# Signs that come in through a rectifier's slope, four early units as 64-token visits, and a new order of work, in a retention and feed-forward kernel

## The chip, the cores and the metric

The kernel runs on one core of a Trainium2 chip. The metric is the device time of one execution in microseconds (us), as the median of several runs. The engines are TensorE (PE, with its weight loads shown apart as PEld), VectorE (DVE), ScalarE (ACT), GpSimd (POOL) and SyncE (SP), which here only issues DMAs.

## The reference

A linear attention with decay (retention) over 8 batches, 8 heads, 576 tokens and a head width of 64 is followed by a feed-forward block with a rational activation.

```python
scores = (1 / sqrt(64)) * q @ k.T                      # per batch and head
ret    = scores * where(i >= j, gamma[h] ** (i - j), 0)
x      = (ret @ v) -> [4608 tokens, 512]
h      = x @ w_in                                      # [4608, 2048]
P      = a0 + a1*h + a2*h**2 + a3*h**3
Q      = 1 + |b0|*|h| + |b1|*h**2
out    = (P / (Q + 1e-6)) @ w_out                      # [4608, 512]
```

Attention's inputs are float32. The weights w_in and w_out come as float64 (512 KB a tile); the host only views them as 64-bit integers, and the chip turns each into float32.

## The kernel before, in words

**Tiles.** The 4608 tokens are 36 units of 128 tokens; four units make a block of 512 columns, of which there are 9. The hidden width 2048 is 16 tiles (`f`). One *step* is one pair (block b, tile f), 144 in all, in the order: block 0 with f = 0 to 7, block 1 with f = 0 to 15, block 0 with f = 8 to 15, then blocks 2 to 8. A step's first product (`gemm1`, `h<-xhi,w` and `h<-xlo,w` in the trace, 12 matmuls of 512 columns) makes h; some fifteen elementwise instructions on ACT, DVE and POOL make g = P/Q from it; the second product (`gemm2`, `acc<-w,g`, 12 matmuls) adds g times w_out to an accumulator. Numbers are split in a high and a low part (`xhi`, `xlo`; `w`; `g`), and three of the four partial products are taken.

**Weights.** There are 32 weight tiles (16 of w_in, 16 of w_out, 512 KB each as loaded). `weight()` (lines 262 to 311) converts one: `begin` (ACT) takes the upper word's magnitude scaled as a float32, `digit` (ACT) takes some bits of the lower word, `join` (DVE) shifts and ors them, `sign` (DVE) ors the sign bit in, `high_part` (ACT or DVE) and `low_part` (POOL or DVE) make the two parts. The tiles w_in 0 to 7 and w_out 0 to 7 are needed by steps 0 to 7, the others from step 16 on.

**Attention.** Units 0 to 7 (`EARLY`) are done by `attention()` (lines 398 to 507): 16 score matmuls of 128 columns (`ps<-qk`), a mask over 1024 columns on DVE (`s<-ps,mask_sb`), outputs (`ps<-s,kv`), the state's update (`ps<-kv`) and the old state's share (`ps<-qk,S_sb`). ACT and DVE then keep the result as `xhi` and `xlo`, DVE adds to the state (`S_sb`) and POOL fades it. From unit 8 on a unit is done by `late_visit()` (lines 631 to 709) in two pieces of 64 tokens: the *visit* after unit n computes unit n's outputs and, interleaved with them on the four quarters of the array, unit n+1's scores and state update.

**Order.** Nothing is emitted in the order of the source. Every piece is a `Task` with a due time, an engine (some have a choice of two, with a `HOLD` penalty), a cost and the buffers it takes. `Plan.run()` (lines 121 to 190) repeatedly picks, by a model of the engines' clocks, the task that can begin first, within a `SLACK` the one that is due first, and emits it. The tables of numbers at the top (`LOADS`, `DUE`, `HOLD`, `SLACK`, `FIRST`, `UNITS`, `LATE`) thus set each engine's queue; `LOADS` sets the order of the first DMAs on SP. Each engine runs its queue in order. `WARM` matmuls on zeros (`unread`) run before the first scores. In the first 24 steps (`IN_BANK`) v's line is kept in the PSUM bank of h; `V_POOL` lists the steps whose `v_mul` goes to POOL.

All instructions show line 71 in the trace (the wrapper that emits them), so they are told apart by their tiles.

Of the kernel before, what the change touches and what calls it, by code (L numbers as in the profile page):

```python
# [22 lines left out]
P = 128  # L23
# [23 lines left out]
LOADS = 'w0 0 gq mask 1 w1 gv 2 w2 3 w4 w5 w3 5 4 ab w7 6 w9 w6 w10 w8 7 w11'.split()
# [8 lines left out]
DUE = {'p_begin': 0.5, 'size': 0.727, 'p_mul': 0.7, 'p_mul2': 0.93, 'v_line': 0.797, 'v_mul': 0.806, 'log': 1.578, 'exp': 1.838, 'quot': 1.6, 'check': 1.65, 'better': 0.79, 'g_hi': 1.888, 'g_lo': 2.167, 'gemm2': 3.44, 'begin': -0.243, 'digit': 0.045, 'join': 0.128, 'sign': -0.303, 'high_part': 1.252, 'low_part': 0.8, 'scale_q': -0.354, 'scale_v': -0.5, 'scores': 0.178, 'decay': 0.311, 'outputs': 1.268, 'cross': 0.51, 'keep_hi': 1.415, 'keep_lo': 0.942, 'grow': 0.669, 'fade': 0.87}  # L56
HOLD = {('POOL', 'scale_v'): 3.0, ('DVE', 'p_begin'): 0.616, ('DVE', 'high_part'): 0.5, ('DVE', 'g_hi'): 1.221, ('DVE', 'keep_hi'): 1.153, ('DVE', 'g_lo'): 99.0, ('DVE', 'low_part'): 1.002, ('POOL', 'v_mul'): 0.229}
SLACK = {'PE': 0.19, 'ACT': 0.283, 'DVE': 0.2, 'POOL': 0.006, 'SP': 0.301}

ADJ = {}  # L60

# [39 lines left out]
class Plan:  # L101
# [19 lines left out]
    def run(self):  # L121
# [14 lines left out]
        dma, left, now, reach = 0.0, len(self.tasks), -2.0, REACH  # L136
        while left:
            best = None
            for e, queue in wait.items():
                found = []  # L140
                for t in queue:
# [8 lines left out]
                    s = max(s, clock[e])  # L150
# [43 lines left out]
def retention_ffn(ctx: ExitStack, tc: tile.TileContext, qkv, w_in, w_out, ab, masks, masks2, gq, gv, out):  # L194
# [8 lines left out]
    cnt = ctx.enter_context(tc.tile_pool(name="cnt", bufs=CNT))  # L203
# [13 lines left out]
        "qk": 2, "kv": 2, "xp": 2, "cnv": CNV, "t": CNT, "v": 2, "u": 2, "p": 3, "g": 3, "o0": 1, "o1": 1,  # L217
# [12 lines left out]
    qc = const.tile([P, 1], F32, name="qc")  # L230
# [27 lines left out]
    bits, parts, joins = {}, {}, []  # L258
# [3 lines left out]
    def weight(order, s, w, f, loaded):  # L262
# [7 lines left out]
        def begin():  # L270
            c_[0] = cnv.tile([P, DM], I32, tag="c", name=f"c{nm}")
            act.activation(c_[0].bitcast(F32), words()[1].bitcast(F32), AF.Abs, scale=math.ldexp(1.0, -112))

        def digit():
            c_[1] = cnt.tile([P, DM], I32, tag="t", name=f"t{nm}")
            act.activation(c_[1], words()[2], AF.Copy, scale=15 * 2.0**-17)

        def join():
            dve.scalar_tensor_tensor(c_[0], c_[0], 3, c_[1], ALU.logical_shift_left, ALU.bitwise_or)

        def sign():
            dve.scalar_tensor_tensor(c_[0], words()[1], -0x80000000, c_[0], ALU.bitwise_and, ALU.bitwise_or)
# [16 lines left out]
        def low_part_v():  # L299
# [3 lines left out]
        t = add("ACT", d + DUE["begin"], 0.55, begin, [loaded], [("cnv", k)])  # L303
        t = add("ACT", d + DUE["digit"], 0.55, digit, [t], [("t", k)])
        t = add("DVE", d + DUE["join"], 0.61, join, [t], [], [("t", k)], True)
        joins.append(t)
        t = add("DVE", d + DUE["sign"], 0.61, sign, [t], shared=True)
        hi = add("ACT", d + DUE["high_part"], 0.53, high_part, [t], other=[("DVE", 0.5, high_part_v, True)])
        w_ready[k] = hi, add(
            "POOL", d + DUE["low_part"], 1.21, low_part, [hi], [], [("cnv", k)], True, [("DVE", 0.61, low_part_v, True)]  # L310
# [20 lines left out]
    def load_unit(n, due, after=()):  # L331
# [4 lines left out]
        def of(w, nm):  # L336
# [12 lines left out]
            add("SP", due + 0.01 * w, 524 / 390.0, of(w, nm), after, [] if late else [(nm, n)])  # L349
# [9 lines left out]
    def scale(n, at_, got, consts):  # L359
# [16 lines left out]

    def attention(n, d, gap, got, consts, prev):
# [121 lines left out]
        th = add("ACT", at_(DUE["keep_hi"]), 0.5, keep_hi, done, [("xp", b)] if n % 4 == 0 else [], gives,  # L499
# [518 lines left out]
```

## Time and profile before

| | |
|---|---|
| median of 3 runs | 900.45 us (900.18 to 901.44) |
| span of the profiled execution | 898.8 us (its own time beside the span is not given; the median is 1.65 us longer than the span) |
| PE busy | 882.9 us, 98% |
| DVE / ACT / POOL busy | 788.7 / 652.5 / 163.3 us |
| DMA rate, first three slices of 22.5 us | 343, 406, 407 GB/s; 82 in the fourth |
| granted TensorE clock | 0.999 on the mean |

Busy time is the time in which an engine has an instruction under way. The time lines have a start and a length in us, then engine, operation, written and read tiles, and a count. In square brackets stands the idle time of the engine just ahead and what ended it. A float32 matmul appears as two instructions, so counts are twice those of the source for some shapes.

### The profile page before, as it was taken

Reading aid. Unit: us, or ns where it says so; the run is one execution under the profiler, and the core shown is the slowest. Engines: PE = TensorE matmul, PEld = TensorE weight load, DVE = VectorE, ACT = ScalarE, POOL = GpSimd, SP = SyncE. Lnnn points to the kernel's source line nnn. Section 1 sums busy time; section 2 is a strip of 40 time slices with the busy share of each in tenths; the row PEclk is TensorE's granted clock in tenths of the full one; section 3 lists DMA queues with packets and bytes.
Section 4 is the critical chain, followed back from the end, with each engine's and each line's share of the span. In section 5 each row is a group of like instructions: output and inputs, shape, how many; then the busy total and the mean of one; then the engine's idle time right before and its main releaser. Section 6 shows DMA issues by size and latency. Waiting matters only on the chain.

```text
span 898.8 us, 17725 instructions
## 1 busy us (share of the span) xinstructions
PE 882.9 (98%) x7344; PEld 730.4 (81%) x7344; DVE 788.7 (88%) x1215; ACT 652.5 (73%) x1019; POOL 163.3 (18%) x141
## 2 busy tenths in 40 slices
PE   6999999999999999999999999999999999999998
PEld 5777888888888888888888888888888888888886
DVE  4899999989989998988988888988888888987976
ACT  3589999975667768666766676767676786767765
POOL 2565664522210110011111010001100000000000
PEclk9999999999999999999999999999999999999999
DMA  9992000034311112111211131112211121001001
GB/s 343 406 407 82 1 1 1 1 107 131 105 49 60 53 34 76 41 47 60 95 48 48 59 107 48 48 47 73 81 48 42 27 80 44 1 1 47 1 1 47
DMA packets 22641, 67.41 MB, mean 75 GB/s; under 512 B 2592, under 2 KB 4512, under 8 KB 22560
## 3 DMA queue, kind: packets, MB, share of 16 engines
q1 hardware_dynamic: 22560, 66.28, 20.8%
q8 instruction: 57, 0.93, 0.4%
q14 instruction: 24, 0.20, 0.1%
HBM read 56.83 MB, written 9.44 MB: 74 GB/s over the span
## 4 chain that ended last, share of the span: by engine, by line
PE 94%; DMA 3%; DVE 2%; issue 0%; SPq 0%; ACT 0%; ACTq 0%; DVEq 0%
PE acc L71 44%; PE h L71 43%; PE ps L71 7%; DMA qk<-in_qkv 1%; DMA bits<-in_w_in 1%; DMA gq_sb<-in_gq 1%; DVE p L71 0%; DVE c L71 0%; DVE s L71 0%; DVE xlo L71 0%; DVE w L71 0%; DVE h L71 0%; DVE kv L71 0%; SPq L71 0%; DVE S_sb L71 0%
## 5 line engine op out<-in xcount | busy, mean ns | idle before, releaser
L71 PE MATMUL acc<-w,g 128*128 128x512 f32 x1632 | 394.1, 390 | 0.0
L71 PEld LDWEIGHTS acc<-w,g 128*128 128x128 f32 x1632 | 305.5, 188 | 64.2 <-POOL w L71 0.4
L71 PE MATMUL h<-xhi,w 128*128 128x512 f32 x1152 | 310.5, 392 | 0.3 <-DVE p L71 0.2
L71 PEld LDWEIGHTS h<-xhi,w 128*128 128x128 f32 x1152 | 213.9, 188 | 46.7 <-DVE p L71 1.3
L71 ACT ACTIVATE p<-h,ab_sb 128x512 f32<-128x512 f32 x143 | 110.7, 774 | 86.3 <-PE h L71 84.5
L71 PE MATMUL h<-xlo,w 128*128 128x512 f32 x576 | 154.2, 389 | 0.0
L71 DVE TENSOR_TENSOR p<-p,h 128x512 f32<-128x512 f32 x144 | 98.4, 683 | 55.7 <-ACT u L71 52.7
L71 DVE SCALAR_TENSOR_TENSOR p<-p,ab_sb,h 128x512 f32<-128x512 f32 x168 | 124.6, 744 | 10.6 <-ACT u L71 8.0
L71 PEld LDWEIGHTS h<-xlo,w 128*128 128x128 f32 x576 | 108.1, 188 | 23.0
L71 ACT ACTIVATE g<-p 128x512 fp32r<-128x512 f32 x136 | 85.6, 630 | 50.8 <-DVE p L71 48.3
L71 ACT ACTIVATE u<-v,qc 128x512 f32<-128x512 f32 x120 | 86.7, 723 | 44.7 <-DVE v L71 44.7
L71 ACT ACTIVATE v<-u,absb 128x512 f32<-128x512 f32 x124 | 101.1, 815 | 3.6
L71 DVE SCALAR_TENSOR_TENSOR p<-p,ab_sb,u 128x512 f32<-128x512 f32 x120 | 93.8, 782 | 4.3 <-ACT u L71 4.3
L71 ACT ACTIVATE u<-h 128x512 f32<-128x512 f32 x144 | 84.8, 589 | 11.1 <-DVE v L71 5.3
L71 DVE SCALAR_TENSOR_TENSOR p<-v,p 128x512 f32<-128x512 f32 x120 | 84.4, 703 | 3.8
L71 DVE SCALAR_TENSOR_TENSOR v<-v,u 128x512 f32<-128x512 f32 x120 | 87.1, 726 | 0.0
L71 DVE TENSOR_TENSOR v<-v,u 128x512 f32<-128x512 f32 x120 | 82.8, 690 | 4.3 <-ACT v L71 3.2
L71 DVE TENSOR_TENSOR g<-p,g 128x512 fp32r<-128x512 f32 x112 | 77.5, 692 | 3.8 <-ACT g L71 2.9
L71 ACT ACTIVATE u<-u 128x512 f32<-128x512 f32 x120 | 75.0, 625 | 2.1
L71 POOL TENSOR_TENSOR qk<-qk,gq_sb 128x512 f32<-128x512 f32 x36 | 49.6, 1379 | 92.5 <-DMA qk<-in_qkv 83.9
L71 PEld LDWEIGHTS ps<-qk 64*64 64x64 f32 (+1 forms) x1024 | 38.1, 145 | 19.8 <-issue 10.8
L71 PE MATMUL ps<-qk 64*64 64x64 f32 (+1 forms) x1024 | 43.6, 234 | 8.1 <-POOL qk L71 6.0
(58 smaller groups left out, 738.4 us busy)
## 6 DMA issues: line engine op xcount, KB each, us to landing
qk<-in_qkv SPq DMA_DIRECT2D x36, 512.0 KB, 4.2
kv<-in_qkv SPq DMA_DIRECT2D x36, 512.0 KB, 5.6
bits<-in_w_in SPq DMA_DIRECT2D x16, 512.0 KB, 10.0
bits<-in_w_out SPq DMA_DIRECT2D x16, 512.0 KB, 10.2
out<-o SPq DMA_DIRECT2D x14, 512.0 KB, 3.3
out<-o SPq DMA_DIRECT2D x8, 256.0 KB, 2.2
x<-in_qkv SPq DMA_DIRECT2D x7, 256.0 KB, 5.3
gq_sb<-in_gq SPq DMA_DIRECT2D x1, 256.0 KB, 6.7
```

What stands on the lines that cost most here:

```text
L71: return lambda *a, **k: self.tc.keep_in_program_order(method(*a, **k))
```

## The change

1. **Weights** (`weight`). `begin` becomes a parametric rectifier in place on the upper words: positive words are scaled by 2^-112 as before, negative ones by a further slope of -2^32, which sets a bit that the later shift by 3 moves to the sign's place. `digit` writes in place over the lower words. `join` reads both from `bits`, writes the new tile `c`, and `sign` is gone: one DVE integer instruction a tile where there were two. The buffer `t` of `digit` is gone.
2. **Units 4 to 7** are no longer done by `attention()` but by `late_visit()`, with the accumulators' PSUM banks (`psa`, `psb`) as their room. Only units 0 to 3 (`DENSE`) stay as they were. Between visits to units 3 and 7 the state passes as in the later visits. Unit 7's visit computes outputs only, unit 8's first visit scores only, as before.
3. **Fewer pointers.** `log` takes its bias as a number and not from the tile `qc`; in the first 24 steps `p_begin` and the line of v lose their bias pointer, and a DVE instruction that follows adds the term instead.
4. **Order.** All tables are new; q/k and k/v of an early unit are placed apart in the order of loads; the planner's model of DMA is changed. `WARM` is 18 instead of 8, `V_POOL` has 9 steps instead of 4.

```diff
-V_POOL = range(4)
+DENSE = 4
+VISITS = (-77.42, -41.32, -7.31, -33.57, -0.9)
+V_POOL = (0, 1, 2, 3, 10, 11, 12, 14, 17)
-WARM = 8
+WARM = 18
-LOADS = 'w0 0 gq mask 1 w1 gv 2 w2 3 w4 w5 w3 5 4 ab w7 6 w9 w6 w10 w8 7 w11'.split()
+LOADS = '1 0 mask gq gv 0v 2 1v w1 w0 3 mask2 w2 2v w5 3v 5v w4 4 ab 4v w3 w8 5 6 w11 6v w7 w10 w6 w9 7v 7'.split()
...
         def begin():
+            x = words()[1].bitcast(F32)
+            act.activation(x, x, AF.Prelu, scale=math.ldexp(1.0, -112), alpha=-math.ldexp(1.0, 32))
+
+        def digit():
+            act.activation(words()[0], words()[2], AF.Copy, scale=15 * 2.0**-17)
+
+        def join():
             c_[0] = cnv.tile([P, DM], I32, tag="c", name=f"c{nm}")
-            act.activation(c_[0].bitcast(F32), words()[1].bitcast(F32), AF.Abs, scale=math.ldexp(1.0, -112))
-
-        def digit():
-            c_[1] = cnt.tile([P, DM], I32, tag="t", name=f"t{nm}")
-            act.activation(c_[1], words()[2], AF.Copy, scale=15 * 2.0**-17)
-
-        def join():
-            dve.scalar_tensor_tensor(c_[0], c_[0], 3, c_[1], ALU.logical_shift_left, ALU.bitwise_or)
-
-        def sign():
-            dve.scalar_tensor_tensor(c_[0], words()[1], -0x80000000, c_[0], ALU.bitwise_and, ALU.bitwise_or)
+            dve.scalar_tensor_tensor(c_[0], words()[1], 3, words()[0], ALU.logical_shift_left, ALU.bitwise_or)
...
-    def visit(n):
+    def visit(n, old, new):
         m, heads = n + 1, [(j, g) for j in range(2) for g in range(NPAIR)]
-        if "ps" not in late_s:
+        if m <= EARLY and not (new and m == EARLY):
+            if "early" not in late_s:
+                late_s["early"] = [ps_acc.tile([P, 2, 512], F32, tag="acc", name=f"ps{x}") for x in "ab"]
+                bank["o"], bank["ds"] = late_s["early"][0][:, 0], late_s["early"][0][:, 1]
+            if new:
+                bank["s"] = late_s["early"][1][:, m % 2]
+        elif "ps" not in late_s:
...
-            act.activation(e["p"], hs[key], AF.Identity, bias=a2, scale=a3)
+            if early:
+                act.activation(e["p"], hs[key], AF.Copy, scale=a3)
+            else:
+                act.activation(e["p"], hs[key], AF.Identity, bias=a2, scale=a3)
...
-            dve.tensor_tensor(p, p, hs[key], ALU.mult)
+            if early:
+                dve.scalar_tensor_tensor(p, p, a2, hs[key], ALU.add, ALU.mult)
+            else:
+                dve.tensor_tensor(p, p, hs[key], ALU.mult)
...
-            act.activation(e["r"], e["v"], AF.Ln, bias=qc)
+            act.activation(e["r"], e["v"], AF.Ln, bias=QC)
...
-    for n in range(EARLY):
-        attention(n, FIRST[n], 2, got[n], consts, prev)
+    for n in range(DENSE):
+        masked.append(attention(n, FIRST[n], 2, got[n], consts, prev))
+    late_s["S0"] = S_sb
+    consts["mask2"] = load(begin_of("mask2"), 32, mask2_sb, masks2)
+    prev = {"fade": prev["fade"]}
+    for n in range(DENSE - 1, EARLY):
+        late_visit(n, VISITS[n + 1 - DENSE], got.get(n + 1), consts, prev, masked[-1:] if n < DENSE else [],
+                   n >= DENSE, n + 1 < EARLY)
```

Three places in the engines' queues follow. In the names the figure behind the letters is the unit (`qk5`), block and tile (`h0_1` is block 0, f = 1; `w0_1` is w_in, f = 1, `c1_0` is w_out, f = 0).

PE where the first step begins, before:

```order
L71 MATMUL ps3_309<-qk3_143,S_sb_105 64x128 x8
L71 MATMUL ps5_404<-qk5_157 128x128 x8
L71 MATMUL h0_0_414<-xhi0_251,w0_0_152 128x512 x4
L71 MATMUL h0_0_414<-xlo0_252,w0_0_152 128x512 x4
L71 MATMUL ps4_432<-qk4_161 128x128 x8
L71 MATMUL ps5_404<-s5_424,kv5_159 64x128 x8
L71 MATMUL ps5_404<-kv5_159 64x64 x8
L71 MATMUL h0_0_414<-xhi0_251,w0_0_152 128x512 x4
L71 MATMUL ps4_432<-s4_461,kv4_173 64x128 x8
```

PE at the same place now:

```order
L73 MATMUL ps3_262<-qk3_142,S_sb_104 64x128 x8
L73 MATMUL h0_0_370<-xhi0_216,w0_0_309 128x512 x4
L73 MATMUL h0_0_370<-xlo0_217,w0_0_309 128x512 x4
L73 MATMUL psb_390<-qk4_237 64x64 x16
L73 MATMUL psa_389<-kv4_256 64x64 x8
L73 MATMUL h0_0_370<-xhi0_216,w0_0_309 128x512 x4
L73 MATMUL h0_1_428<-xhi0_216,w0_1_239 128x512 x4
L73 MATMUL h0_1_428<-xlo0_217,w0_1_239 128x512 x4
L73 MATMUL psb_390<-qk5_298 64x64
```

The first step's product now follows unit 3 at once, and units 4 to 7 come as visits of 64-column matmuls between the first products of steps 0 to 5.

DVE from the masks of units 2 and 3 to the low part of unit 3's result, before:

```order
L71 TENSOR_TENSOR s2_304<-ps2_282,mask_sb_98 128x1024
L71 TENSOR_TENSOR s3_339<-ps3_309,mask_sb_98 128x1024
L71 TENSOR_TENSOR kv3_145<-kv3_145,gv_sb_100 128x512
L71 SCALAR_TENSOR_TENSOR c0_2_266<-c0_2_266,t0_2_297 128x512
L71 TENSOR_TENSOR S_sb_105<-S_sb_105,ps2_282 128x256
L71 TENSOR_TENSOR xlo0_252<-ps2_282,xhi0_251 128x4x128
L71 SCALAR_TENSOR_TENSOR c0_2_266<-bits0_2_140,c0_2_266 128x512
L71 SCALAR_TENSOR_TENSOR c1_0_341<-c1_0_341,t1_0_377 128x512
L71 TENSOR_TENSOR S_sb_105<-S_sb_105,ps3_309 128x256
L71 TENSOR_TENSOR xlo0_252<-ps3_309,xhi0_251 128x4x128
```

The same stretch of DVE's queue now:

```order
L73 TENSOR_TENSOR s3_274<-ps3_262,mask_sb_98 128x1024
L73 SCALAR_TENSOR_TENSOR c0_0_296<-bits0_0_140 128x512
L73 TENSOR_TENSOR kv3_193<-kv3_193,gv_sb_100 128x512
L73 SCALAR_TENSOR_TENSOR c0_2_311<-bits0_2_146 128x512
L73 TENSOR_TENSOR S_sb_104<-S_sb_104,ps2_241 128x256
L73 TENSOR_TENSOR xlo0_217<-ps2_241,xhi0_216 128x4x128
L73 TENSOR_TENSOR kv5_197<-kv5_197,gv_sb_100 128x512
L73 SCALAR_TENSOR_TENSOR c1_0_354<-bits1_0_222 128x512
L73 SCALAR_TENSOR_TENSOR c0_4_358<-bits0_4_170 128x512
L73 TENSOR_TENSOR S_sb_104<-S_sb_104,ps3_262 128x256
L73 TENSOR_TENSOR xlo0_217<-ps3_262,xhi0_216 128x4x128
```

Each weight tile has one instruction here where it had two, but four tiles are joined in this stretch instead of parts of two, and unit 5's v is scaled ahead of unit 3's result.

ACT's first instructions, before:

```order
L71 ACTIVATE c0_0_132<-bits0_0_117 128x512
L71 ACTIVATE t0_0_136<-bits0_0_117 128x512
L71 ACTIVATE w0_0_152<-c0_0_132 128x512
L71 ACTIVATE c0_1_198<-bits0_1_129 128x512
L71 ACTIVATE t0_1_205<-bits0_1_129 128x512
L71 ACTIVATE xhi0_251<-ps0_164 128x4x128
```

ACT's first instructions now:

```order
L73 ACTIVATE bits0_1_138<-bits0_1_138 128x512
L73 ACTIVATE xhi0_216<-ps0_149 128x4x128
L73 ACTIVATE bits0_1_138<-bits0_1_138 128x512
L73 ACTIVATE bits0_0_140<-bits0_0_140 128x512 x2
L73 ACTIVATE w0_1_239<-c0_1_225 128x512
L73 ACTIVATE xhi0_216<-ps1_161 128x4x128
```

The first weight is no longer converted ahead of the attention; unit 0's and unit 1's results stand behind weight instructions.

## Rows read from the trace of the kernel before

**Rows 1.** The page, busy time of each engine, and the DMA rate by slice

```profile
PE 882.9 (98%) x7344; PEld 730.4 (81%) x7344; DVE 788.7 (88%) x1215; ACT 652.5 (73%) x1019; POOL 163.3 (18%) x141
...
GB/s 343 406 407 82 1 1 1 1 107 131 105 49 60 53 34 76 41 47 60 95 48 48 59 107 48 48 47 73 81 48 42 27 80 44 1 1 47 1 1 47
```

**Rows 2.** Busy time by stretch: length, PE, PEld, DVE, ACT, POOL, clock, DMA share, GB/s

```profile
100.00:165.00 65.00, 65.00 (x289) 53.83 (x288) 63.60 (x98) 64.09 (x110) 37.95 (x28) 1.00 0.00 1
165.00:285.00 120.00, 119.40 (x1318) 98.59 (x1319) 109.50 (x172) 84.07 (x137) 26.34 (x23) 1.00 0.22 74
```

**Rows 3.** The chain of waits in order of time: start, length, what

```profile
85.81 2.72 PE h L71 x12
```

**Rows 4.** Time line from the start to the first step's product

```profile
1.06 3.79 PE L71 MATMUL unread<-S_sb 128*128 128x128 f32 x16 [1.06 <-DVE qc L71]
...
4.25 0.66 ACT L71 ACTIVATE c<-bits 128x512 f32<-128x512 f32 x1 [2.22 <-DMA bits<-in_w_in]
...
8.93 1.26 POOL L71 TENSOR_TENSOR qk<-qk,gq_sb 128x512 f32<-128x512 f32 x1 [8.47 <-DMA gq_sb<-in_gq]
...
10.24 4.24 PE L71 MATMUL ps<-qk 64*128 64x128 f32 x32 [5.39 <-POOL qk L71]
...
12.37 1.23 DVE L71 TENSOR_TENSOR s<-ps,mask_sb 128x1024 f32<-128x1024 f32 x1 [4.01 <-PE ps L71]
...
31.00 0.68 DVE L71 TENSOR_TENSOR xlo<-ps,xhi 128x512 fp32r<-128x512 f32 x1
...
31.35 1.20 PE L71 MATMUL h<-xhi,w 128*128 128x512 f32 x4
```

**Rows 5.** Time line of PE: one early unit, and where step 8 begins

```profile
46.96 1.09 PE L71 MATMUL ps<-s,kv 128*64 128x128 f32 x16
47.88 0.64 PE L71 MATMUL ps<-kv 128*64 128x64 f32 x16
48.45 1.16 PE L71 MATMUL ps<-qk 64*128 64x128 f32 x16
49.54 1.09 PE L71 MATMUL ps<-qk,S_sb 64*64 64x128 f32 x16
50.56 1.20 PE L71 MATMUL h<-xhi,w 128*128 128x512 f32 x4
...
79.05 1.98 PE L71 MATMUL h<-xhi,w 128*128 128x512 f32 x8
```

**Rows 6.** Time line of PE: first and second late visit

```profile
183.66 1.15 PE L71 MATMUL ps<-qk 64*64 64x64 f32 x32
...
185.21 2.11 PE L71 MATMUL acc<-w,g 128*128 128x512 f32 x8
187.25 0.27 PE L71 MATMUL ps<-qk 64*64 64x64 f32 x1
...
189.28 1.19 PE L71 MATMUL acc<-w,g 128*128 128x512 f32 x4
```

**Rows 7.** DVE by operation: tiles, shape, count, busy us, mean ns, idle before

```profile
L71 DVE TENSOR_TENSOR xlo<-ps,xhi 128x512 fp32r<-128x512 f32 x36 | 24.6, 683 | 1.6 <-ACT xhi L71 1.5
L71 DVE SCALAR_TENSOR_TENSOR c<-bits,c 128x512 int32<-128x512 int32 x32 | 22.9, 717 | 0.2
L71 DVE TENSOR_TENSOR kv<-kv,gv_sb 128x512 f32<-128x512 f32 x32 | 22.7, 711 | 1.3 <-DMA kv<-in_qkv 0.9 <-DMA gv_sb<-in_gv 0.2
...
L71 DVE TENSOR_TENSOR s<-ps,mask_sb 128x1024 f32<-128x1024 f32 x7 | 8.5, 1218 | 4.3 <-PE ps L71 4.3
...
L71 DVE TENSOR_TENSOR S_sb<-S_sb,ps 128x256 f32<-128x256 f32 x6 | 2.5, 415 | 2.7 <-ACT xhi L71 1.4 <-PE ps L71 1.3
```

**Rows 8.** ACT by operation, as in rows 7

```profile
L71 ACT ACTIVATE u<-v,qc 128x512 f32<-128x512 f32 x120 | 86.7, 723 | 44.7 <-DVE v L71 44.7
...
L71 ACT ACTIVATE u<-u 128x512 f32<-128x512 f32 x120 | 75.0, 625 | 2.1
...
L71 ACT ACTIVATE c<-bits 128x512 f32<-128x512 f32 x32 | 21.3, 667 | 11.5 <-DMA bits<-in_w_in 8.2 <-DVE w L71 2.1 <-POOL w L71 1.1
```

More of the change, by code (lines that the diff above doesn't have):

```diff
@@ L135, in run @@
         port = {"DVE": 0.0, "POOL": 0.0}
[L136 removed]
+        dma, landed, left, now, reach = 0.0, [0.75] * OUTSTANDING, len(self.tasks), -2.0, REACH
         while left:
@@ L254, in retention_ffn @@
     first = half + NF
-    bits, parts, joins = {}, {}, []
+    bits, parts = {}, {}
     need = sorted(((at[1, f] if f >= half else f) + 3 * w, w, f) for w in range(2) for f in range(NF))
@@ L302, in weight @@
         d = min(s - LEAD, AHEAD + order)
[L303 to L308, printed above, removed]
+        t = add("ACT", d + DUE["begin"], 0.56, begin, [loaded])
+        t = add("ACT", d + DUE["digit"], 0.56, digit, [t])
+        t = add("DVE", d + DUE["join"], 0.6, join, [t], [("cnv", k)], shared=True)
+        hi = add("ACT", d + DUE["high_part"], 0.52, high_part, [t], other=[("DVE", 0.5, high_part_v, True)])
         w_ready[k] = hi, add(
-            "POOL", d + DUE["low_part"], 1.21, low_part, [hi], [], [("cnv", k)], True, [("DVE", 0.61, low_part_v, True)]
+            "POOL", d + DUE["low_part"], 1.25, low_part, [hi], [], [("cnv", k)], True, [("DVE", 0.6, low_part_v, True)]
         )
@@ L498, in attention @@
         gives = [("acc", key)]
-        th = add("ACT", at_(DUE["keep_hi"]), 0.5, keep_hi, done, [("xp", b)] if n % 4 == 0 else [], gives,
+        th = add("ACT", at_(DUE["keep_hi"]), 0.495, keep_hi, done, [("xp", b)] if n % 4 == 0 else [], gives,
                  other=[("DVE", 0.6, keep_hi_v, False)])
@@ L622, in named, with late_visit @@
         return emit
-    def late_visit(n, d, got, consts, prev, hold):
-        old, m = n >= EARLY, n + 1
-        new, u = m < NU, (n + 1) % 9
+    def late_visit(n, d, got, consts, prev, hold, old=True, new=True):
+        m, u = n + 1, (n + 1) % 9
+        early = m <= EARLY and not (new and m == EARLY)
         tq = tv = None
@@ L646, in late_visit @@
         if m in sooner:
-            tm = add("DVE", d - 1.5, 0.42, named(middle, m), [prev["visit"], prev.get("fade")])
+            tm = add("DVE", d - 1.5, 0.33, named(middle, m), [prev["visit"], prev.get("fade")])
         if n + 2 in sooner:
@@ L662, in late_visit @@
         ts = add(
-            "PE", d, (1.7 if m in sooner and n % 9 != 8 else 2.2) if old and new else 1.2, named(visit, n),
+            "PE", d, (1.7 if m in sooner and n % 9 != 8 else 2.2) if old and new else 1.2, named(visit, n, old, new),
             [tq, tv, tm, te, *hold, *(prev.get(x) for x in ("decay", "middle", "grow", "lo", "before"))],
-            [("h", key)] if new else [],
+            [("acc", "va"), ("acc", "vb")] if early and not old else [("h", key)] if new and not early else [],
         )
```

138 lines of the change are left out of this document (72 added, 66 removed).

## The prediction

> **What bounds the kernel now.** I read the busy times first. PE has work under way for 882.9 of 898.8 us [rows 1], and from step 8 on the chain of waits lists little but PE pieces like the one in [rows 3]: 12 products of 512 columns in 2.72 us, one after the other. So time can be won only by giving PE less to do, or where PE is not full. The table by stretch says where that is not: from 100 to 165 us PE is busy for 65.00 of 65.00, and from 165 to 285 us for 119.40 of 120.00 [rows 2]. In the first of these ACT (64.09) and DVE (63.60) are full as well, so anyone who makes PE arrive earlier must ask whether they can follow. What is left is the start, and there I read the time line. PE's first scores start at 10.24, behind POOL's scaling of q at 8.93, which waited for the DMA of gq; the first step's product starts only at 31.35, behind unit 3's result (its low part is made by DVE at 31.00) [rows 4]. Step 8 starts at 79.05 + 4 x 2.72/12 = 79.96, since the eight products of that row are four of step 7 and four of step 8 [rows 5].
>
> Between 31.35 and 79.96 lie 48.6 us. The work in them: 8 first products and 4 second ones, 12 x 2.72 = 32.6, and units 4 to 7. A unit's pieces start at 46.96, 47.88, 48.45, 49.54 and the next at 50.56 [rows 5]: outputs 0.92, state 0.57, scores 1.09, old state 1.02, in all 3.6. Four make 14.4; unit 4 has its old state on half its columns (0.5 less) and one set of scores (1.1) was done ahead of 31.35, so 12.8. Work 45.4, gaps 3.2.
>
> **Part 1, the head (to the first step's product).** The DMAs run at about 0.28 MB/us from 4.25 us, when the first 0.52 MB are there, to 8.93, when gq closes 1.84 MB (three loads of 512 KB and its own 256), and at the page's 406 GB/s later [rows 1, 4]. With the new loads gq closes 1.48 MB (two of 512 KB, the mask's 160, its own): 4.25 + 0.95/0.28 = 7.7, so 1.2 us sooner, and the first scores start near 9.0.
> The 18 warming products cost nothing or little: 8 of them take 3.79 us [rows 4], 18 at that pace 8.5, to 9.6 us, 0.55 later than 9.0; the pace may rise on the way. I take nothing, since DVE's queue, below, ends later.
> Of the clock: the granted clock of these rows is full, yet the 32 scores from 10.24 took 4.24 us [rows 4], where 16 later take 1.16 [rows 5]. [...]
> DVE's queue from the first mask (12.37) to the end of unit 3's low part (31.68) is 19.3 us [rows 4]. It holds 4 masks at 1.22, 4 v scalings and 4 low parts at 0.70, 4 state updates at 0.42 [rows 7] and five weight instructions, priced like the sign at 0.72: 15.8, so 3.5 of waits. Now it starts with a v scaling (0.71) as soon as unit 0's v is there (2.01 MB, 9.4 us), and holds 4 masks, 5 scalings, 4 low parts, 4 updates and 5 joins: 4.9 + 3.6 + 2.7 + 1.7 + 3.6 = 16.5. Each tile is one instruction cheaper (0.72), but five are joined before unit 3 is kept. With no wait it would end at 25.9, with the old waits at 29.4. Following it by hand against the loads gives the place between: w1 lands at 13 to 13.7 and stands on ACT ahead of unit 0's result, and w0's two instructions (0.67 each [rows 8]) ahead of unit 1's, so unit 1's low part ends at 18.9; mask, v, mask, join, v, join of units 2 and 3 follow without a gap to 24.2 (unit 3's v, 6.76 MB, is there at 21.1); unit 2's state and low part 25.3; unit 5's v and two joins 27.6; unit 3's state and low part 28.8. I take 28.8. PE can start the first step on the high part at 27.9, and waits for the low one, as if it had started at 27.9 without a wait: **31.35 - 27.9 = 3.4 us** (0.5 more to 6, to 2.8).
>
> **Part 2, units 4 to 7 as visits.** A half visit with scores only takes 185.21 - 183.66 = 1.55, a full one 189.28 - 187.25 = 2.03 [rows 6]. Now: one half (1.55), three full (6.1), and one with outputs only, which no row shows; its 32 matmuls cost between the 1.0 of half as many and the 2.03 of a full visit, taken as 1.5. Sum 9.1 against 12.8: **3.7 us**. The bounds of the last half make it 3.1 to 4.2.
>
> **Part 3, gaps up to step 8.** 3.2 us before. A visit must wait for the mask (0.68), two state sums (0.42 each) and the low part (0.68) of the one before, 2.2 in one DVE queue plus ACT's high part; PE has 12 to 16 products, 2.7 to 3.6 us, in between. Three hand-offs fit. At step 4's product I find a wait: its bank is freed by step 0's last DVE instruction, which stands behind step 0's exponential on ACT, and that behind step 2's first two ACT instructions: 1.3 us. Six changes between visits and products at about 0.2 add 1.2. **2.6 against 3.2: 0.6 us**, taken as 0.5; if the wait at step 4 hides, 1.9, and if two more come, 2 us of loss.
>
> **Part 4, what lies beside PE.** Sign: 32 x 0.72 = 22.9 us of DVE go. Pointers: a logarithm with its pointer takes 723 ns, the exponential without one 625 [rows 8]; 144 logarithms and some 39 early instructions at 0.1 each are 18 us less on ACT, and DVE pays 24 x 0.06 for the added term. Neither is worth anything at PE from step 8 on, where PE has no gap; their use is that PE can come 7 us sooner without outrunning them. From the first instruction of step 4 to that of step 24 ACT's queue has 174 instructions where it had 191; at 64.09/110 = 0.58 us each [rows 2] that is 101 us against PE's 20 x 5.44 = 109, so ACT keeps up.
> Rectifier and digit in place: writes to every second word are not in the trace. Reading so costs nothing above a plain pass to 0.05 us (667 against 625 ns, [rows 8]); I take 0, with 64 x 0.05 = 3 us of ACT as the upper end, under ACT's 8 us of room, and a gain is excluded, as no fewer elements pass. If cover is gone the cost lies in part 1, where ACT stands before unit 0's and 1's results: 0.2.
> DMAs: the same bytes; unit 7's q and k are the last an early visit needs, 15.2 MB, at 8.93 + 13.4/0.406 = 41.9 us, and 1.3 of POOL after; its visit starts at 44.6. v products on POOL, 9 instead of 4: 5 x 1.4 us on an engine that is busy for 37.95 of 65 [rows 2]. From step 8 to the end PE's work is the same, and most visits stand before a second product where they stood behind it. I take 0, between -0.6 (the gap of 165 to 285 [rows 2] goes) and +1.
>
> **Sum.** 3.4 + 3.7 + 0.5 = 7.6 us off the span: 898.8 - 7.6 = 891.2, and with the 1.65 us by which the median of the runs exceeds the span, 892.8.
>
> **Rivals.**
> *A. Hand-offs between visits fail.* If each of the four costs the 1.3 us that I find once, 3.9 us more are lost: 896.7. For it: the DVE queue is in order, and after each visit it holds two to five instructions of steps and weights beside the 2.2 us. Against it: those stand ahead of the mask and run while the visit does.
> *B. The head is as fast as its data and the gaps close.* DVE ends at 25.9 instead of 28.8 (2.9), or at half that with the 1.3 us at step 4 hidden and 0.6 after 165 us: 3.4 more, 889.4. Against it: w1 and w0 on ACT hold up units 0 and 1 whatever DVE does.
> *C. The later visits pay: slower.* About 26 visits of units 9 to 35 now stand right behind a first product, and need one of the two h banks; if PE waits there for the step before to release its bank, the loss is paid at every visit. At 0.3 us each the gain is gone (900.6), from 0.37 on the kernel is slower; at 0.45 it is 26 x 0.45 - 7.6 = 4.1 slower, 904.5. Against it: the bank's last reader has 2 x 2.72 us, and its four elementwise instructions need about 2.8; DVE has 10.5 of 120 us free in 165 to 285 [rows 2].
> *D. The rectifier is no plain ACT pass.* If it needed its own table, or wrote slowly, ACT would lose more than its room of 8 us over 64 instructions, from 0.13 us each on, and PE would wait between steps 4 and 24. At 0.2 us that is 12.8 - 8 = 4.8 us: 897.6. The queue shows one table load as before, which speaks against the first.
>
> **Chances.** Forecast (gain 5 to 10) 0.62, A and D together (gain 2 to 5) 0.17, B (more than 10) 0.08, C 0.13, of which half within 0.2%. A measurement of this kernel can tell 0.2%, 1.8 us, from no change. So faster 0.87, same 0.06, slower 0.07. The range reaches from B's 889 less a little to the weaker end of A and D: 888.0 to 898.0.
>
> **What would show it.** Right: the first step's product near 28 us; unit 3's low part as its releaser; step 8 near 72 us; PE without gaps from there, and a step pair still 5.44 us; no instruction `c<-bits,c`; rectifier near 0.67 us. Wrong in part 1 if the step starts after 30; in part 2 if a visit takes over 2.4; in part 3 if PE idles over 4 us between first product and step 8; C if four steps with a visit take well over 4 x 5.44 + 2.03 = 23.8 us. A rectifier above 0.8 us makes it D.

## The result, and the profile after

The changed kernel takes 910.50 us (median of 4 runs, 908.72 to 912.38), the one before beside it 900.75: ratio 1.0108, 95% interval 1.0091 to 1.0124. It is 1.1% slower, where 892.8 us was forecast. The profiled execution took 912.38 us, its span is 910.6, against 898.8 before. It is the slowest of the four, so the rows below hold up to 1.9 us that the median does not have.

The page's busy times, where [rows 1] stood for before, and the two stretches of [rows 2]:

```profile
PE 887.6 (97%) x7588; PEld 732.7 (80%) x7588; DVE 791.4 (87%) x1182; ACT 626.8 (69%) x1017; POOL 168.2 (18%) x143
```

```profile
100.00:165.00 65.00, 64.02 (x282) 52.39 (x281) 58.33 (x78) 59.98 (x107) 39.05 (x30) 1.00 0.00 1
165.00:285.00 120.00, 115.38 (x1197) 94.75 (x1196) 107.81 (x165) 78.68 (x128) 25.08 (x22) 0.97 0.22 74
```

ACT has 25.7 us less work, as intended, and from 100 to 165 us ACT and DVE are idle for 5.0 and 6.7 us. Yet PE, full before, now misses 0.98 of those 65 us and 4.62 of the next 120 (0.60 before), at a mean granted clock of 0.97. So PE stands more than before, although the engines beside it were relieved.

The head's time line, against [rows 4]:

```profile
1.05 7.21 PE L73 MATMUL unread<-S_sb 128*128 128x128 f32 x36 [1.05 <-DVE S_sb L73]
...
8.90 1.76 DVE L73 TENSOR_TENSOR kv<-kv,gv_sb 128x512 f32<-128x512 f32 x1 [7.91 <-DMA kv<-in_qkv]
8.94 2.39 PE L73 MATMUL ps<-qk 64*128 64x128 f32 x32 [0.68 <-POOL qk L73]
...
20.13 1.12 DVE L73 TENSOR_TENSOR kv<-kv,gv_sb 128x512 f32<-128x512 f32 x1 [0.81 <-DMA kv<-in_qkv]
21.31 1.98 PE L73 MATMUL ps<-s,kv 128*64 128x128 f32 x16 [1.19 <-DVE kv L73]
23.07 1.07 PE L73 MATMUL ps<-kv 128*64 128x64 f32 x16
...
25.99 0.42 DVE L73 TENSOR_TENSOR S_sb<-S_sb,ps 128x256 f32<-128x256 f32 x1 [1.80 <-ACT xhi L73]
...
27.64 2.29 DVE L73 SCALAR_TENSOR_TENSOR c<-bits 128x512 int32<-128x512 int32 x2
...
28.95 1.20 PE L73 MATMUL h<-xhi,w 128*128 128x512 f32 x4 [0.70 <-ACT xhi L73]
30.19 0.68 DVE L73 TENSOR_TENSOR xlo<-ps,xhi 128x512 fp32r<-128x512 f32 x1
30.92 1.20 PE L73 MATMUL h<-xlo,w 128*128 128x512 f32 x4 [0.77 <-DVE xlo L73]
```

The first scores start 1.3 us sooner and take 2.39 us instead of 4.24. The first step begins at 28.95, with its low part at 30.92: as if it had started at 30.0 without a wait, against 31.35 before and 27.9 forecast. Where the 2 us went is worked out below (part 1).

PE between there and step 8, against [rows 5]:

```profile
47.21 0.98 PE L73 MATMUL h<-xhi,w 128*128 128x512 f32 x3 [1.61 <-issue]
...
53.76 0.21 PE L73 MATMUL psa<-qk,S 64*64 64x64 f32 x1 [1.82 <-issue]
...
55.31 1.91 PE L73 MATMUL h<-xlo,w 128*128 128x512 f32 x4
...
75.50 0.74 PE L73 MATMUL h<-xhi,w 128*128 128x512 f32 x2 [0.79 <-ACT w L73]
...
81.12 1.07 PE L73 MATMUL h<-xhi,w 128*128 128x512 f32 x4
```

Two gaps have no releaser ("issue"): one behind the first pass of step 3's product, one in the middle of a visit. Behind the second, four passes of 512 columns take 1.91 us where they take 1.07 elsewhere; the granted clock of 50 to 60 us is 0.83. Step 8 begins at 81.12, 1.2 us later than before.

The first late visit, against [rows 6]:

```profile
182.36 1.15 PE L73 MATMUL ps<-qk 64*64 64x64 f32 x32 [2.50 <-DVE p L73]
185.15 1.12 PE L73 MATMUL ps<-kv 64*64 64x64 f32 x16 [1.65 <-DVE p L73]
186.20 2.07 PE L73 MATMUL acc<-w,g 128*128 128x512 f32 x4
188.07 1.91 PE L73 MATMUL h<-xhi,w 128*128 128x512 f32 x4
```

PE waits 4.15 us for a bank whose last reader is DVE's `p`, and then works at half speed until 191.6, at a granted clock of 0.50 from 184.8 to 191.4 us. By operation, against [rows 7, 8]:

```profile
L73 DVE SCALAR_TENSOR_TENSOR c<-bits 128x512 int32<-128x512 int32 x32 | 32.2, 1020 | 0.0
...
L73 ACT ACTIVATE u<-v 128x512 f32<-128x512 f32 x120 | 75.1, 626 | 24.6 <-DVE v L73 23.0
...
L73 ACT ACTIVATE bits<-bits 128x512 f32<-128x512 f32 x64 | 39.6, 667 | 14.3 <-DMA bits<-in_w_in 14.3
```

Rectifier and digit take 667 ns on the mean, as the absolute value did before, and a logarithm 626 instead of 723. The sign is gone, but the join that is left has a mean of 1020 ns.

### The profile page after: what moved, and what is told of

Read it like the earlier page. It is cut to its first block, busy times and chain, and to the rows that moved or that the text cites. A ratio compares the mean times of both kernels' runs of the same rounds, so it can differ in the third digit from the quotient of the medians.

```text
span 910.6 us, 18269 instructions
## 1 busy us (share of the span) xinstructions
PE 887.6 (97%) x7588; PEld 732.7 (80%) x7588; DVE 791.4 (87%) x1182; ACT 626.8 (69%) x1017; POOL 168.2 (18%) x143
## 4 chain that ended last, share of the span: by engine, by line
PE 77%; DVE 8%; ACT 7%; DMA 3%; issue 3%; POOL 1%; SPq 0%; ACTq 0%; DVEq 0%; POOLq 0%
PE acc L73 36%; PE h L73 35%; PE ps L73 6%; DVE p L73 4%; DMA kv<-in_qkv 3%; ACT bits L73 2%; DVE c L73 2%; ACT u L73 1%; ACT p L73 1%; ACT h L73 1%; DVE v L73 1%; DVE kv L73 1%; DVE g L73 0%; DVE h L73 0%; DMA out<-o 0%
## 5 line engine op out<-in xcount | busy, mean ns | idle before, releaser
L73 PEld LDWEIGHTS h<-xhi,w 128*128 128x128 f32 x1152 | 216.6, 189 | 49.6 <-issue 2.0
L73 DVE SCALAR_TENSOR_TENSOR p<-p,ab_sb,h 128x512 f32<-128x512 f32 x192 | 142.1, 743 | 15.7 <-ACT u L73 10.7
L73 DVE TENSOR_TENSOR p<-p,h 128x512 f32<-128x512 f32 x120 | 82.2, 685 | 54.4 <-ACT u L73 52.9
L73 PEld LDWEIGHTS h<-xlo,w 128*128 128x128 f32 x576 | 109.0, 190 | 24.2 <-DVE xlo L73 1.4
L73 ACT ACTIVATE v<-u,absb 128x512 f32<-128x512 f32 x129 | 105.0, 814 | 2.4
L73 DVE SCALAR_TENSOR_TENSOR p<-v,p 128x512 f32<-128x512 f32 x120 | 93.3, 777 | 3.5
L73 ACT ACTIVATE u<-v 128x512 f32<-128x512 f32 x120 | 75.1, 626 | 24.6 <-DVE v L73 23.0
L73 POOL TENSOR_TENSOR qk<-qk,gq_sb 128x512 f32<-128x512 f32 x36 | 51.8, 1441 | 112.2 <-DMA qk<-in_qkv 105.0
L73 ACT ACTIVATE bits<-bits 128x512 f32<-128x512 f32 x64 | 39.6, 667 | 14.3 <-DMA bits<-in_w_in 14.3
L73 PEld LDWEIGHTS ps<-qk 64*64 64x64 f32 (+1 forms) x960 | 32.7, 138 | 17.1 <-issue 10.5
```

The source lines that it names most:

```text
L73: return lambda *a, **k: self.tc.keep_in_program_order(method(*a, **k))
```

## The experiments

Two kinds of change are held apart here: what is computed, and the order that the planner makes of it. Times are medians; the kernel before stood at 900.7 to 901.0 in each group.

**e1: the weight conversion alone.** The kernel before with rectifier, digit and join of the changed kernel; the planner sets the order anew.

```diff
-            act.activation(c_[0].bitcast(F32), words()[1].bitcast(F32), AF.Abs, scale=math.ldexp(1.0, -112))
+            act.activation(x, x, AF.Prelu, scale=math.ldexp(1.0, -112), alpha=-math.ldexp(1.0, 32))
...
-        t = add("DVE", d + DUE["sign"], 0.61, sign, [t], shared=True)
```

> The kernel before with the new weight conversion alone (sign by the rectifier's slope, one join a tile), its tables, dense units and pointers kept. Theory 1, the loss sits in the new order of work and in units 4 to 7: this one is free of it, 899 to 901 us, and the relief of DVE is worth nothing because PE had no gap. Theory 2, the new join itself costs (1.02 us each in the profile of the changed kernel, since it stands still while POOL works): elementwise work falls behind as in the changed kernel, 903 us or more, with PE waits around 180 us.

907.78 us, ratio 1.0081 (1.0064 to 1.0097). Theory 1 fails. Time and waits stand where theory 2 put them, but e10 will show that the new join is not the reason. A kernel with 32 DVE instructions less is 7 us slower. PE waits where it did not before, among others:

```profile
181.21 0.96 PE L71 MATMUL h<-xhi,w 128*128 128x512 f32 x3 [1.13 <-DVE p L71]
...
186.84 1.15 PE L71 MATMUL ps<-qk 64*64 64x64 f32 x32 [1.71 <-DVE p L71]
```

**e2: all of the change but early visits and tables.** `DENSE = 8`, tables of before.

> The changed kernel's code with all eight early units dense again and with the tables, V_POOL and WARM of before: weights, pointers and the planner's model of DMA are new, order and units are as before. Theory 1: 899 to 902 us. Theory 2: 903 us or more. A gain of more than 2 us would say that fewer pointers are worth something by themselves.

919.65 us, 1.0211 (1.0188 to 1.0234): theory 1 fails again, and this is the slowest. About half of the loss lies ahead of step 8: the first step begins at 41.06 us for 31.35 before, step 8 is 9.7 us late. Another part is one wait for an accumulator that ACT evicts late:

```profile
115.83 0.80 PE L73 MATMUL acc<-w,g 128*128 128x512 f32 x1 [5.24 <-ACT o L73]
```

**e3: early visits, tables of before.**

```diff
-VISITS = (-77.42, -41.32, -7.31, -33.57, -0.9)
+VISITS = (-20.0, -17.0, -14.0, -11.0, -8.0)
...
-UNITS = (15.817, 3.656, -2.844)
+UNITS = (20.48, 2.58, -2.5)
```

> The changed kernel's code with units 4 to 7 as visits, but with the tables of before (due times of the visits -20, -17, -14, -11, -8). Theory 1, if it is the tables: the 3.7 us of PE work saved by the visits show, 895 to 898 us. If it is the visits (each waits for the one before, and PE's clock falls after each wait): 903 us or more, with granted clock below 0.9 between 30 and 65 us.

903.14 us, 1.0032 (1.0015 to 1.0049). Theory 1 fails: the first step begins at 33.26 us for 31.35 before, a gap without a releaser takes 1.57 us behind it, and PE waits at the first late visit again. The other theory has the time but not its reason, since the granted clock from 30 to 65 us is 1.00.

```profile
181.11 0.68 PE L73 MATMUL ps<-kv 64*64 64x64 f32 x16 [1.84 <-DVE p L73]
...
184.30 1.20 PE L73 MATMUL h<-xhi,w 128*128 128x512 f32 x4 [1.36 <-DVE p L73]
```

**e4: the changed kernel, its first late visit later.** The table sets when the first four late visits are due. PE's order ahead of the first is unchanged; it stands 16 passes of 512 columns further on, four of a second product and 12 of a first one.

```diff
-UNITS = (15.817, 3.656, -2.844)
+UNITS = (26.5, 0.3, -2.844)
```

> The changed kernel with one table entry moved (UNITS from 15.817, 3.656 to 26.5, 0.3): the first late visit stands behind step 26's first product and not within step 25's, so 1.3 steps later; all of PE's queue ahead of it is unchanged. Theory 1, this visit's waits for DVE (2.5 and 1.65 us at 182 us) and the half clock behind them cost 7 us: 902 to 905 us, clock 1.00 between 180 and 195 us. If elementwise work is simply too slow there, the wait comes back at the next visit: 908 to 911 us.

903.25 us, 1.0031 (1.0015 to 1.0047). The 4.15 us of waits are 0.33, no half speed follows, and 910.50 - 903.25 = 7.25 us are back. By the two traces 5.8 of them fall behind step 8 (from the low part of its product to the end 828.6 and 822.8 us, 818.0 before). Up to there, in the same order, e4's execution is 3.0 us faster; its granted clock is 1.00 where the changed kernel's falls to 0.83. The two issue gaps stayed, at the same instructions.

```profile
180.80 1.15 PE L73 MATMUL ps<-qk 64*64 64x64 f32 x32 [0.33 <-DVE p L73]
```

**e5: e4 with four more warming products.** The trace has a DMA queue that carries only instructions. Its row of the page (of the changed kernel: packets, MB, share of 16 engines):

```profile
q8 instruction: 59, 0.97, 0.4%
```

0.97 MB in 59 packets is 16.4 KB each; PE's 7588 passes and as many weight loads, 15,176 instructions, make 257 a packet; in the kernel before 57 packets stand beside 14,688, 258 each. From these counts a packet was taken for a block of PE's instructions, some 128 passes. Two of the 59 blocks came late, if the gaps of 1.61 and 1.82 us are theirs. To test this, the program was shifted (`WARM = 22`).

> The kernel of the later first visit (903.25 us) with 22 instead of 18 warming products: 8 PE passes (16 instructions) more at the start, nothing else. Theory L (PE's instructions arrive in blocks of 16 KB, and PE stops where a block that has not landed begins): both gaps without a releaser keep their length (1.5 to 1.9 us) but move 8 passes toward the start of the program. The first stood behind 5 of the 12 passes of step 3's first product; it now stands one pass into the four that close step 2's first product. The second stood behind 116 of the 128 passes of the visit of unit 6; it now stands behind some 108. The two blocks of the queue for instructions that landed at 43.3 and 49.6 still come 2.5 to 2.7 us ahead of the end of each gap. Rival D (a weight or a state that PE waits for without a row that says so): the gaps stay at the same products, behind 5 of 12 and 116 of 128 passes. Time 901 to 906 by either.

905.62 us in one run. The first gap left step 3's product and now stands 3 recorded passes before the end of the visit ahead of it, 8 recorded passes sooner, as many as were put in. Counted from the start, the first gap stands behind 601 recorded passes in the changed kernel, e4 and e5 alike, the second behind 728 in the changed kernel, e4 and e6. The gap was longer than expected, and the second fell away. Place and data do not make the gap; the count of instructions does.

```profile
47.27 0.27 PE L73 MATMUL psa<-qk,S 64*64 64x64 f32 x1 [2.75 <-issue]
```

Where a window of the trace first holds the packet, and where PE goes on (both us; windows of 0.2 us):

| kernel | packet | PE goes on | between |
|---|---|---|---|
| after | 44.58, 51.05 | 47.21, 53.76 | 2.6, 2.7 |
| e3 | 30.23 | 32.65 | 2.4 |
| e4 | 43.31, 49.64 | 45.89, 52.36 | 2.6, 2.7 |
| e5 | 44.72 | 47.27 | 2.6 |
| e6 | 50.06 | 53.29 | 3.2 |
| e7 | 44.16, 50.20 | 46.58, 52.87 | 2.4, 2.7 |
| e8 | 32.34 | 34.95 | 2.6 |
| e11 | 29.39 | 31.90 | 2.5 |

In e6 the packet itself took 1.6 us, in the others 1.0 to 1.1: from its end to PE's going on it is 1.3 to 1.6 us in each row. The name "issue" alone shows no late block: e2 has such a gap of 1.87 us at 39.65, with no packet between 31.5 and 46 us, and it ends 0.1 us behind DVE's low part of a unit.

**e6 and e9: e4 with a pause in the loads.** Four (e6) or nine (e9) tiny copies, each waiting for the last, ahead of the thirteenth weight tile in the queue of loads.

```diff
...
+            if k == 12:
+                for x in range(CHAIN):
+                    sp.dma_start(pause[:, (x + 1) % 2 : (x + 1) % 2 + 1], pause[:, x % 2 : x % 2 + 1])
```

> The kernel of the later first visit (903.25 us), with four tiny copies within SBUF, each waiting for the one before, in the queue of loads ahead of the thirteenth weight tile. They hold the loads back for some 8 to 15 us from about 35 us on, so that the DMAs run empty between about 45 and 52 us. Theory L: a block of instructions then lands sooner behind the one before (3 to 4 us instead of 6.2 to 7.2), the second gap (1.78 us at 52.36) is gone or under 0.4, the first (1.70 at 45.89) shrinks as far as the queue is already empty then (0 to 1.7), and step 4 runs at full clock; 899.5 to 902. Rival D: the gaps stay at 1.7 and 1.8 us, and the time at 903 or, where held loads come too late for the weights, above.

> The kernel with the loads' pause, with nine copies in its chain instead of four, so that the loads stop from about 34.8 to about 55 us (four held them to 47.64) and the DMAs are empty from some 43 to 56 us. In the run with four the first gap without a releaser was gone (its block of instructions came 4.5 us behind the one before), but the second stood at 1.54 us, with its block at 50.06, 1.5 us behind the loads' return. Theory L (blocks of instructions are late because the loads fill the DMAs): that block now comes by 48.5 us, and the second gap is gone too (under 0.3 us); if the weights that land later are not waited for, 899.5 to 901.5. Rival F (a block takes PE 6 us or more whatever the loads do, and the first gap went for another reason): the second gap stays between 1.2 and 1.9 us; 901.5 to 904.

e6 901.84 us, 1.0012 (1.0001 to 1.0024): the first gap is gone (its block came 4.5 us behind the one before, instead of 7.2), the second is 1.54 us. e9 902.29, 1.0015 (1.0004 to 1.0025), with the second down to 0.17 too; DMA share 0.05 from 43 to 55 us, where it is 1.03 in the changed kernel. First e6, then e9:

```profile
53.29 0.21 PE L74 MATMUL psa<-qk,S 64*64 64x64 f32 x1 [1.54 <-issue]
```

```profile
50.47 0.27 PE L74 MATMUL psa<-s,kv 64*64 64x64 f32 x2 [1.09 <-DVE xlo L74]
...
52.60 0.21 PE L74 MATMUL psa<-qk,S 64*64 64x64 f32 x1 [0.17 <-issue]
```

So the loads hold up the block of the first gap. The second gap in e9 proves less: its block came at 49.65, 6.2 us behind the one before and not by 48.5 as theory L had it, and PE came late to the place, after 1.09 us of waiting for the low part on DVE. Without that wait some 1.2 us of gap would stand there (an estimate, 1.09 + 0.17). By the medians e6 and e9 gain 1.4 and 1.0 us over e4, in ranges that overlap, and not the 3.5 of both gaps.

**e7: e4 with `V_POOL = range(4)`.**

> The kernel of the later first visit with 4 instead of 9 v products on POOL (so five more on DVE). Theory P (a DVE instruction with two inputs in SBUF stands while POOL works, so that the joins last 1020 ns instead of some 700): fewer of the steps 8 to 23 have POOL work beside DVE, the mean join falls to 0.90 us or less, the wait at the first accumulator's eviction (0.98 us near 104) goes, 901 to 903. Rival: the joins stay above 0.98 us, since low parts, scalings and fades keep POOL as busy where the joins stand; DVE has 5 x 0.69 us more work, and the time is 903 to 905.

909.67 us, 1.0096 (1.0083 to 1.0109), outside both ranges. Joins do fall, to a mean of 903 ns (968 in e4), and the kernel is 6.4 us slower than e4: the plan came out otherwise, and PE waits 3.22 us for `p` at the first late visit. What shorter joins are worth in a held order is not shown.

```profile
184.94 1.98 PE L73 MATMUL ps<-qk 64*64 64x64 f32 x32 [3.22 <-DVE p L73]
```

**e8: e3 with a later first visit (`UNITS = (26.5, 0.3, -2.5)`).**

> The changed kernel with early visits, but with the order tables of before (903.14 us in its own run), and its first late visit some one and a half steps later (UNITS begins at 26.5 with 0.3 between the first four). In that run PE waited 1.84 and 1.36 us at the first late visit for p on DVE and then ran at half speed for some 3 us. Theory 1 (what the change loses beyond the head is an order in which PE meets instructions that ACT and DVE have not finished): these 6 us go, 896 to 898.5, faster than both kernels. Rival: the visits now stand in another place where p is not ready either, or the four first ones, close together, wait for each other: 900 to 903.

905.43 us, 1.0047 (1.0033 to 1.0061), outside both ranges. The table entry that won 7 us in e4 here puts the visit 28 passes further on, and the wait moves and grows (3.20 us in e3):

```profile
192.65 2.01 PE L73 MATMUL h<-xhi,w 128*128 128x512 f32 x4 [4.54 <-DVE p L73]
```

**e10: e1 with the order of before kept.** The planner books the sign's time and nothing is issued for it; PE, POOL and SP are instruction by instruction as before.

```diff
...
-        t = add("DVE", d + DUE["sign"], 0.61, sign, [t], shared=True)
+        t = add("DVE", d + DUE["sign"], 0.61, lambda: None, [t], shared=True)
```

> The kernel before with the new weight conversion alone, and with the order of before kept: the planner still books the sign's 0.61 us on DVE and places the rest around it, but nothing is issued there. PE, POOL and SP have instruction by instruction the order of before, DVE the same without its 32 signs, ACT the same with rectifier and digit in place of absolute value and digit. With the order set anew the same conversion took 907.78 us (PE waits of 1.40, 1.16, 1.13 and 1.71 us, ACT and DVE 7 us idle each between 85 and 172 us). Theory O (the new order, not the new instructions, loses the time): no PE wait over 0.6 us between 30 and 200 us, 898.5 to 901.5, within 0.2% of before. Rival I (the new instructions lose it: joins of some 0.9 to 1.0 us instead of 0.72 to 0.84 on the path of each tile): the waits at 170 to 187 us come back, 903 or more.

899.56 us, 0.9982 (0.9973 to 0.9991), faster than before. This is e1's arithmetic, 8.2 us faster by order alone. Busy times from 85 to 172 us, columns as in [rows 2]; first before, then e1, e10 and the changed kernel:

```profile
85.00:172.00 87.00, 87.00 (x385) 72.07 (x384) 85.29 (x132) 85.96 (x148) 49.28 (x37) 1.00 0.00 1
```

```profile
85.00:172.00 87.00, 85.33 (x372) 69.11 (x372) 79.70 (x117) 79.50 (x136) 44.60 (x36) 1.00 0.00 1
```

```profile
85.00:172.00 87.00, 87.00 (x385) 72.08 (x384) 82.83 (x117) 86.30 (x149) 48.79 (x37) 1.00 0.00 1
```

```profile
85.00:172.00 87.00, 86.02 (x379) 70.61 (x378) 77.44 (x107) 78.90 (x140) 53.14 (x39) 1.00 0.00 1
```

Read the third and fourth busy time, DVE and ACT. In e10 ACT is busy for 86.3 of 87 us, in e1 for 79.5 with the same work at hand: the 7 us are idle time, ACT waiting for DVE's `p` and DVE for ACT's `u`. In this stretch ACT waits 7.3 us for DVE and DVE 6.2 us for ACT in e1, 0.4 and 2.2 us in e10. The largest waits of e1 (us in total, times, longest):

```profile
ACT u L71 <- DVE p L71: 4.7, 8, 1.4
DVE p L71 <- ACT u L71: 4.7, 8, 0.7
```

The changed kernel looks like e1, with 7.1 and 8.4 us. Its joins are not slower than e10's (1144 ns in this stretch there, 1044 here).

**e11: e3 with the sign's time booked.** As in e10, nothing is issued for it.

> The changed kernel with early visits and the tables of before (903.14 us in its own run, with waits of 1.84 and 1.36 us for p on DVE at 181 to 184 us), with 0.61 us per weight tile booked on DVE in the planner's model and nothing issued for it, so that the plan sees DVE later. Theory O: a plan that books what the chip really takes (joins of 0.98 us for the 0.6 booked) places the visits where p is ready; the waits at 181 us fall to under 1 us together, 897 to 901. Rival: the early visits and their instruction gaps cost what they win, and the plan meets other waits: 901.5 to 906.

902.68 us, 1.0017 (1.0008 to 1.0026). The waits at 181 us fall to 0.46, as theory O said, and the time lands where the rival said, through a late weight and an instruction gap:

```profile
31.90 0.30 PE L73 MATMUL psa<-kv 64*64 64x64 f32 x3 [1.91 <-issue]
...
74.39 1.75 PE L73 MATMUL h<-xhi,w 128*128 128x512 f32 x4 [2.52 <-ACT w L73]
```

**e12: e10 with the change's arithmetic of the steps (fewer pointers), order still kept.**

```diff
...
-            act.activation(e["r"], e["v"], AF.Ln, bias=qc)
+            act.activation(e["r"], e["v"], AF.Ln, bias=QC)
```

> The kernel of the kept order (new weights, order of before, 899.56 us, 0.9982 of before) with the third part of the change added, the arithmetic of the feed-forward steps with fewer pointers, again without moving an instruction: a logarithm takes 626 instead of 690 to 723 ns, the early line 689 instead of 780. Theory O: from step 8 on PE has no wait that ACT or DVE could shorten, so 144 cheaper logarithms on ACT give nothing: 898.8 to 900.3, the same as without them; the waits between 30 and 200 us stay under 0.6 us. Rival: ACT was close to holding PE up (86.3 of 87 us busy between 85 and 172 us), and its some 8 us of relief take 1 us or more off PE: under 898.6. Other rival: DVE pays for the added terms and p comes later, 901 or more.

899.18 us, 0.9984 (0.9975 to 0.9993): the same as e10, as theory O said. ACT now waits 2.2 us for PE in that stretch, and PE has no gap in it. e10 and e12 are the versions that beat both kernels, by 1.3 and 1.6 us against the one before.

## Why the prediction was wrong

The span came out at 910.6 where the sum said 891.2: 19.4 us. 8.8 are lost by step 8 (81.12 against 31.35 - 3.4 + 44.4 = 72.3), 10.6 behind it. These are rows of the slowest execution; by the medians the forecast is off by 17.7 us.

*Part 1 (3.4 us, came to 1.35).* The data came as worked out: `gq` released POOL at 7.62 us for 7.7 forecast, the scores at 8.94 for 9.0. DVE's queue also kept its time at first: the last join ahead of unit 2's result ends at 24.19 for 24.2, although two v scalings took 1.76 and 1.12 us for 0.71. The step that failed is that the sum let DVE's queue alone set the end and gave PE's speed no part in it. DVE then stands 1.80 us for ACT's high part of unit 2, since PE's outputs, late by 1.19 us of waiting for the second of these scalings, ran at half speed: 1.98 and 1.07 us for 1.09 and 0.64, some 1.3 us from start to start, at a granted clock of 0.50 from 21.0 to 24.0 us, 0.83 on the mean of 20 to 30. Two joins then took 2.29 for 1.44. Together this is somewhat more than the 2.1 us by which the step is late. e4, in the same order, kept a clock of 1.00 there, and its first step stands as if begun at 28.6; e7, e5 and e6 (0.83) at 29.4, 30.3 and 30.3, e9 (0.66) at 31.0. So by e4 0.7 us are left to the order and DVE; the rest goes with the clock and differs from run to run. Slow joins could be seen before, just ahead of unit 3's result:

```profile
29.00 1.75 DVE L71 SCALAR_TENSOR_TENSOR c<-c,t 128x512 int32<-128x512 int32 x1
```

The prediction also read the granted clock of [rows 4] as full. The trace of before has no entry of it ahead of 16.66 us. In e10, with PE's order of before, it is 0.50 from 8 to 14 us, where 16 scores take 2.08 us. That the 32 scores of [rows 4], 4.24 us, were at such a clock too is argued from this, not shown.

*Part 2 (3.7 us, came to about 2.5).* From start to start and without their waits the visits take 1.55, 2.03, 2.34, 2.34 and 2.01 us, 10.3 for 9.1. The half with outputs only took 2.01 for 1.5: the upper bound of its price, 2.03, was nearly the true value. Two full ones cost 0.3 more than the 2.03 put in, where they were broken by a wait.

*Part 3 (2.6 us of gaps forecast).* This step failed. The waits up to step 8 are 0.34, 1.61, 1.82 and 0.79, 4.56 together; slower work around the gaps costs 2.2 (0.4 at the first, at full clock; 4.5 instead of 2.72 for step 4's product, at half speed); what is left for changes is some 1.4, where 1.2 was forecast (six at 0.2 us, an estimate that no row showed). The wait found by hand at step 4 did not show. What was not seen is a resource the argument never listed: PE's own instructions. A dense unit of [rows 5] has 64 passes in 3.6 us, a visit has 128 in 2, about one block, and beside the loads (DMA share 1.03) the blocks came 6.3 to 7.1 us apart. e5 shows that the gaps go by instruction count, e6 that the first goes when the loads rest; for the second that is argued. Why they come so far apart, and why PE goes on only some 2.5 us behind the packet, is left open.

*Part 4 ("I take 0").* The largest error, 10.6 us. That PE has no gap from step 8 on in [rows 2] was taken as a property of the work; it was one of the order. The sum counted how many instructions ACT has (174 for 191) and not when each one waits for DVE. In the new order each of them waits for the other (the rows under e10), and where a visit takes one of the two `h` banks PE stands. At the first late visit the trace shows 7.3 us of the 10.6, 4.15 of waits and 3.2 of half speed (186.20 to 191.60 us for 12 passes, and the update ahead of them); e4, which moves it, gives back 7.25 by the medians and 5.8 by the traces. 0.98 at an accumulator's eviction (106.56 us) and 1.15 us behind 400 us stand in the trace, the other 1.2 are not traced to rows. That the two engines' waits for each other bring PE's is argued; that the order does, and not the arithmetic, is shown by e1 and e10. That arithmetic is worth nothing beside PE was right when the order is kept: from the low part of step 8's product to the end the kernel before takes 818.0 us, e10 818.4 and e12 817.9, and what these two gain lies ahead of it.

*The rivals.* C had the right place, PE waiting for an `h` bank at late visits, and the wrong size: 26 equal prices of 0.45 us were reckoned, and it is one visit, the first, with 4.15 us of waits. It got 0.13. A named hand-offs between visits; they cost 0.34. D is refuted by the rectifier's 669 ns (digit 666). B did not come near.

*The chances.* Slower had 0.07, half of C, since every other rival only takes some of the gain back. A change of all tables at once is a new plan, and e1, e2, e3 and e8 show what a new plan does here: 903 to 920 us, all slower, with the same or less work.

## What to carry to other kernels

Where a planner sets the order, take arithmetic away first with the order held (book the old time, issue nothing), and measure the new order by itself. An engine's busy share says how much work it has, not how late it runs: look for mutual waits of two elementwise engines, and for the first place where the full engine needs a bank from them. When work is cut into smaller instructions, count instructions a microsecond as well as columns (here 128 passes in 2 us for 64 in 3.6), above all while loads fill the DMAs (share 1.03 here).

## What the runs showed of the hardware

- PE has 15,176 instructions where the queue for instructions has 59 packets, 14,688 for 57 before: blocks of about 257, if all of them are PE's (an estimate). Beside loads at 0.41 MB/us the changed kernel's came 6.3 to 7.1 us apart from 37.5 to 57.5 us, where the visits lie, and PE stopped for 1.5 to 2.75 us (the changed kernel, e4, e5, e6); with the loads at rest (e6, e9) they came 4.1 to 6.2 us apart, and the longest stop was 0.17.
- Three waits of the changed kernel were followed by matmuls that took up to twice as long: 1.98 for 1.09 us behind a wait of 1.19, four passes in 1.91 for 1.07 behind 1.82, 2.07 and 1.91 behind 1.65. The granted clock is 0.50 there, from 21.0 to 24.0, 55.1 to 58.3 and 184.8 to 191.4 us (0.83 on the mean of 20 to 30 and of 50 to 60). In e4 the gap of 1.78 us was not followed by it, nor in e6 that of 1.54 (clock 1.00 from 50 to 60 us in both). So a wait cost its length in these, and in the three two to three times that: 1.3 us of slower work stand behind the 1.19, 1.8 behind the 1.82, 3.2 behind the 1.65.
- A join on DVE takes 0.68 us or, as at 176.46 us in the changed kernel, 1.82; a scaling of v 0.68 or 1.76. In the changed kernel's trace 16 joins and scalings took over 0.9 us, and each had POOL work beside it for 0.57 us or more; the 41 with none took 0.68 to 0.69, but some with up to 0.8 us of it took no more than 0.78. That POOL is the cause is argued from this, and e7, with fewer POOL products and joins of 903 for 968 ns, points the same way; it was not tried by itself.
- A rectifier with a negative slope, in place and over every second word, takes 669 ns, an absolute value over every second word 667.
